# Moved weight steps, gate and fills, and fewer zero matmuls, in the first rounds of an RWKV and Sinkhorn-MoE kernel

## The chip, the cores and the metric

The kernel runs on one core of a Trainium2 chip. The metric is device time in microseconds (us) of one execution of the whole program. Besides the plain runs there is one profiled execution, from which every row below comes. Its engines are TensorE (PE, its weight loads PEld), VectorE (DVE), ScalarE (ACT), GpSimd (POOL) and SyncE (SP), whose queue issues most of the DMA transfers.

## What is computed

Attention in the RWKV manner over `r`, `k`, `v` of shape (4, 8, 768, 48), and on its output `x` of shape (3072, 384) a mixture of 8 experts whose gate is normalised by 8 Sinkhorn steps:

```python
for t in range(S):
    cur = einsum('bhd,bhe->bhde', u * k[t], v[t])
    y[t] = einsum('bhd,bhde->bhe', r[t], state + cur)
    state = w * state + einsum('bhd,bhe->bhde', k[t], v[t])
x = y as (3072, 384)
logits = x @ w_gate
P = exp(logits - logits.max())
for _ in range(8):
    P /= P.sum(1, keepdims=True) + 1e-9
    P /= P.sum(0, keepdims=True) + 1e-9
    P *= N / E
out = sum over e of P[:, e] * (relu(x @ w1[e]) @ w2[e])
```

## The kernel before, in words

The program has an attention part of 27 rounds (the loop at L720, `i` from 0), in which the 24 tiles of 128 tokens pass a software pipeline, and then 14 stages for experts 1 to 7. From the sixth round on (`i` = 5) TensorE also works on expert 0: `units` is a list of groups of matmuls that `work` (L693) takes one by one. In rounds 1 to 5 there are no units yet, and `work` issues three zero matmuls instead (`spin`, L286: 128x512, f16, into a PSUM tile that nobody reads, `pz`). Everything is issued in program order: `InOrder` (L21) keeps each engine's instructions in the order in which the Python code calls them, so the order of the calls is the order on every engine's queue.

What a round `i` does, by function:

- `load_chunk(i + 4)` puts three loads on SP's queue (`rn`, `kn`, `vn`, 192 KB each). `prep(i + 2)` (L477) scales r on POOL (`rp`) and k on VectorE (`kp`). `bonus_dot(i + 1)` (L483) is two products on POOL, r times k and that times u (`rk`).
- `stage_b(i + 1)` (L500) transposes `rp` and `kp` on TensorE (`prT`, `pkT`); ScalarE copies them out (`rT`, `kT`).
- `scale_x(i - 2)` scales an output tile on ScalarE (`xsc`). `bonus(i)` (L490) is a reduction on VectorE (`dg`) and two products on POOL, the second of which reads `hbx`.
- `stage_c(i)` (L511) makes the scores on TensorE (`pA`), which VectorE copies through a mask into `at`, and the state's update (`pu`, then `S`).
- `stage_e(i - 2, bank_)` (L576) transposes a scaled tile (`px`); ScalarE writes its high half into `hbx` (a CAST) and VectorE the low half. `stage_d(i - 1)` (L547) makes the output (`py`); VectorE adds the bonus (`x`) and takes the scale of each row from its maximum (`xm`, `inv_s`, `xs`). `stage_f(i - 3, bank_)` (L584) multiplies by the gate's weights (`px<-wgp,hbx`); VectorE writes `lparts`.

The tiles `prT`, `pkT`, `pA`, `pu` and `py` share four PSUM banks in turn (pool `ps3`), so a round's second `pA` tile takes the bank of an earlier `py` and must wait until VectorE has read that for `x`.

Between these the round places the preparation of expert 0's weights: `split_weights` (L151) gives a list of steps, and `STEPS` (L708) says how many of them `prepare` (L689) takes after `stage_c` and at the round's end. For w1, and again for w2, they are: three maxima (`amax`, VectorE, `wm`), `reduce_max` (`wma`), an empty step, `across` (a transpose, then a reduction and a small matmul that spreads the maximum over the partitions), an empty step, `scale` (`isw`, `sw`), and for each of three pieces a high half on ScalarE (`high`: `ws<-ws,sw`, 128x1024) and a low half on VectorE (`low`: `ws<-ws,sw,ws`). The gate's weights `wg` pass the same steps once: `gate_max` (`wgm`), `gate_across`, `gate_split` (`iswg`, `swg`, then `wgp` on ScalarE and VectorE).

Before the loop, the two `at` tiles are cleared on POOL (L355), part of `hbx` is zeroed on ScalarE (L334), and a branch (L409) on a flag sends rare decay values down a slow path, which is not taken here. SP issues no load past that branch until the first loads of w1 have landed.

Of the kernel before, what the change touches and what calls it, by code (L numbers as in the profile page):

```python
# [8 lines left out]
F32 = mybir.dt.float32  # L9
# [3 lines left out]
ALU = mybir.AluOpType  # L13
# [19 lines left out]
def rwkv_sinkhorn_moe(  # L33
# [17 lines left out]
    B, H, S, D = r.shape  # L51
# [99 lines left out]
    def split_weights(e, r1, r2, home):  # L151
        w1h = part(home, F16, 0, (KC, F))
        w1l = part(home, F16, KC * F, (KC, F))
        w2h = part(home, F16, 2 * KC * F, (FC, DM))
        w2l = part(home, F16, 2 * KC * F + FC * DM, (FC, DM))
        isw = const.tile([P, 2], F32, name=f"isw_{e}")
        sw = sm.tile([P, 2], F32, tag="sw", name=f"sw_{e}")
        m = sm.tile([P, 2 * KC], F32, tag="wm", name=f"wm_{e}")
        ma_ = [sm.tile([P, 1], F32, tag=f"wma{j}", name=f"wma_{e}_{j}") for j in range(2)]
        res = {}  # L160
        pieces = []

        def rest_():
            pass

        for raw, wh, wl, j in ((r1, w1h, w1l, 0), (r2, w2h, w2l, 1)):
            fl = [x.rearrange("p c f -> p (c f)") for x in (raw, wh, wl)]
            n = fl[0].shape[1] // KC

            def amax(i, fl=fl, j=j, n=n):  # L170
                V.tensor_reduce(
                    m[:, j * KC + i : j * KC + i + 1], fl[0][:, i * n : (i + 1) * n],
                    axis=AX.X, op=ALU.max, apply_absolute_value=True,
                )

            def reduce_max(j=j):
                V.tensor_reduce(ma_[j], m[:, j * KC : (j + 1) * KC], axis=AX.X, op=ALU.max)

            def across(j=j):
                res[j] = over_partitions(ma_[j], 1, ps1, "ph", f"w{e}_{j}")  # L180
                next(res[j])

            def scale(j=j):
                pow2_scale(next(res[j]), isw[:, j : j + 1], sw[:, j : j + 1], 0.25)

            def high(i, fl=fl, j=j, n=n):
                sl = slice(i * n, (i + 1) * n)
                S_.activation(fl[1][:, sl], fl[0][:, sl], AF.Copy, scale=sw[:, j : j + 1])

            def low(i, fl=fl, j=j, n=n):  # L190
                sl = slice(i * n, (i + 1) * n)
                V.scalar_tensor_tensor(
                    fl[2][:, sl], fl[0][:, sl], sw[:, j : j + 1], fl[1][:, sl],
                    op0=ALU.mult, op1=ALU.subtract,
                )

            steps = [lambda i=i, f=amax: f(i) for i in range(KC)] + [reduce_max, rest_, across, rest_, scale]
            for i in range(KC + 1):
                fs = [lambda i=i, f=high: f(i)] if i < KC else []
                fs += [lambda i=i, f=low: f(i - 1)] if i else []  # L200
                if i >= KC - 1:
                    fs.append(lambda i=i, j=j: split_done.add((("w1", "w2")[j], i - KC + 1)))
                steps.append(lambda fs=fs: [f() for f in fs])
            pieces += steps
        return (w1h, w1l, w2h, w2l, isw), pieces
# [113 lines left out]
    for c in range(KC):  # L319
# [11 lines left out]
    V.memset(unit[:, :, 0:1], 1.0)  # L331
    V.memset(step[:, :, 0:1], 0.0)
    V.memset(hbx[:, HB : 2 * HB], 0.0)
    S_.mul(  # L334
        hbx[:, 2 * HB :].rearrange("p (a q) -> p a q", q=HP),
        unit[:, :1, 1:].broadcast_to([P, HB // HP, HP]), 0.0,
    )
    spin(19)
    wbd = ac.tile([P, NPAIR, 2, D], F32, name="wbd")
    G.memset(wbd, 0.0)  # L340
# [11 lines left out]
    at_ = [ac.tile([P, H, C], F32, name=f"at{i}") for i in range(2)]  # L352
    for t_ in rp_ + kp_:
        G.memset(t_[:, :, D:], 0.0)
    for t_ in at_:  # L355
        G.memset(t_, 0.0)

    wlim = part(hb3, F32, 2496, (H, D))[:1]
    flag = ac.tile([1, 1], F32, name="flag")
# [51 lines left out]
            scan_channels(scratch)  # L411

    load_part(1, "v", v)
    load_part(3, "r", r)
    load_part(3, "k", k)
    Q.dma_start(wg, w_gate.rearrange("(c p) e -> p c e", p=P))
    load_part(2, "v", v)
    load_part(3, "v", v)

# [14 lines left out]
    V.tensor_tensor(tab[:, :, HP:], pw[:, :, :HP], gb, op=ALU.mult)  # L434
    V.tensor_tensor(tab[:, :, :HP], iv[:, :, HP:0:-1], gb, op=ALU.mult)
    S_.copy(tabr[:, :, :HP], pw[:, :, HP - 1 :: -1])
    S_.copy(tabr[:, :, HP:], iv[:, :, 1:])
    rtab = ac.tile([P, NPAIR, 2, HP], F32, name="rtab")
    ktab = ac.tile([P, NPAIR, 2, HP], F32, name="ktab")
# [42 lines left out]

    def bonus_dot(tt):  # L483
        ld_ = loads[tt]
        rk = at2.tile([P, H, D], F32, tag="rk", name=f"rk_{tt}", bufs=3)
        G.tensor_tensor(rk, ld_["r"], ld_["k"], op=ALU.mult)
        G.tensor_tensor(rk, rk, ub, op=ALU.mult)
        st[tt]["rk"] = rk

# [203 lines left out]
    def work(n, ready=True):  # L693
        if not ready:
            spin(3)
            return
        for _ in range(n):
            if units:
                whole(units.pop(0))
# [3 lines left out]
    for sg in range(3):  # L703
# [2 lines left out]
        side += steps  # L706

    STEPS = {  # L708
        0: (2, 1), 1: (1, 2), 2: (2, 1), 3: (1, 1), 4: (1, 0),
        5: (1, 1), 6: (2, 2), 7: (3, 1), 8: (1, 1),  # L710
    }

    def n_steps(i):
# [4 lines left out]
    stage_b(0)  # L718
    bonus_dot(0)
    for i in range(NTT + 3):  # L720
        if i == 2:
            gate_max()
        if i + 2 < NTT:
            if i + 4 < NTT:
                load_chunk(i + 4)
            if i == 0:
                Q.dma_start(raws[1], w2[0].rearrange("(c p) d -> p c d", p=P))
            prep(i + 2)
        if i + 1 < NTT:
            bonus_dot(i + 1)  # L730
            stage_b(i + 1)
        if 2 <= i <= NTT + 1:
            scale_x(i - 2)
        work(1, i > 4)
        if i < NTT:
            bonus(i)
            if ("S", i) in st:
                st[i]["S"] = st.pop(("S", i))
            stage_c(i)
        for _ in range(n_steps(i)[0]):  # L740
            prepare()
        if i <= NTT:
            work(2 if i > 8 else 1, i > 4)
        if i == 2:
            gate_res = gate_across()
        if i >= 2:
            bank_ = ps2.tile([P, TB], F32, tag="po", name=f"px_{i}")
        if 2 <= i <= NTT + 1:
            stage_e(i - 2, bank_)
            emitted[0] = i - 1  # L750
        if i > NTT:
            work(2)
        if 1 <= i <= NTT:
            stage_d(i - 1)
        if i == 2:
            gate_split(gate_res)
        for _ in range(n_steps(i)[1]):
            prepare()
        if 3 <= i:
            stage_f(i - 3, bank_)  # L760
        done = i - 2
        if 0 <= done < NTT and done % TH == TH - 1:
            po_ = done // TH
            if po_ == 0:
                units += [g1_unit(0, fc, W) for fc in range(FC)]
                units += [g2_half(0, t, 0, W) for t in range(TH)]
                pend = [(0, t, 1) for t in range(TH)]
            for j in range(2 if po_ else 0):
                g1 = [g1_unit(po_, fc, W) for fc in range(j * FHC, (j + 1) * FHC)]
                g2 = [g2_half(*a, W) for a in pend]  # L770
                units += merged(g1, g2)
                pend = [(po_, t, j) for t in range(TH)]
# [447 lines left out]
```

## Time and profile before

| | |
|---|---|
| runs | 1563.62, 1563.85, 1565.07 us; median 1563.85 us |
| the profiled execution | 1563.49 us, of which the span from first to last instruction is 1561.8 us |
| PE | 1549.8 us busy (99%), 9297 matmuls |
| DVE | 1020.8 us (65%) |
| ACT | 671.9 us (43%) |
| POOL | 589.0 us (38%) |
| chain of waits that ended last | PE 95%, DVE 2%, POOL 1% |
| granted TensorE clock | 1.0 in all 40 slices |

The table is read as one long stretch in which TensorE is never free, with a short beginning in which other engines hold it up. Shares over the whole span hide that beginning: the rows further down look at it by itself.

### The profile page before, as it was taken

What the parts mean: (1) busy time and instruction counts of PE and PEld (TensorE: products, weight loads), DVE (VectorE), ACT (ScalarE), POOL (GpSimd) and SP (SyncE); (2) the same over time, 40 slices, a digit from 0 to 9 for tenths busy, and PEclk for the clock granted to TensorE, in tenths of its full rate; (3) what the DMA queues carried; (4) which work ended last, traced back from release to release, by engine and by line L of the source; (5) the groups of instructions that cost most, each with busy time, mean ns of one, the idle gap of its engine ahead of it and who ended that gap; (6) DMA issues with size and microseconds to landing.
All of it is one profiled execution on the core that took longest, in us unless ns stands there. A gap on an engine that the chain in (4) does not pass through costs nothing.

```text
span 1561.8 us, 24068 instructions
## 1 busy us (share of the span) xinstructions
PE 1549.8 (99%) x9297; PEld 899.0 (58%) x9297; DVE 1020.8 (65%) x1694; ACT 671.9 (43%) x1190; POOL 589.0 (38%) x688
## 2 busy tenths in 40 slices
PE   8999999999999999999999999999999999999999
PEld 5877786655555555555555555555555555555555
DVE  7876674957666676666666666666666656656554
ACT  3433332534444354544444453544444444535320
POOL 8777764620012424243342424242423324242200
PEclk9999999999999999999999999999999999999999
DMA  9333311221215556576766666565545555556434
GB/s 197 68 88 79 84 49 36 98 82 45 92 64 103 79 87 111 85 127 90 128 83 122 86 127 90 93 95 70 86 57 99 57 95 61 96 59 97 56 91 132
DMA packets 167638, 138.26 MB, mean 89 GB/s; under 512 B 90337, under 2 KB 161762, under 8 KB 167522
## 3 DMA queue, kind: packets, MB, share of 16 engines
q0 software_dynamic: 44928, 61.36, 32.6%
q1 hardware_dynamic: 122384, 75.35, 17.4%
q8 instruction: 73, 1.20, 0.3%
q14 instruction: 43, 0.35, 0.1%
q10 hardware_dynamic: 210, 0.00, 0.0%
HBM read 55.39 MB, written 80.23 MB: 87 GB/s over the span
## 4 chain that ended last, share of the span: by engine, by line
PE 95%; DVE 2%; POOL 1%; ACT 0%; issue 0%; DMA 0%; SPq 0%; POOLq 0%; DVEq 0%; ACTq 0%
PE po L29 47%; PE bZ L29 11%; PE bY L29 11%; PE ph L29 5%; PE bA L29 5%; PE bB L29 5%; PE py L29 3%; PE bC L29 2%; PE pA L29 1%; PE pu L29 1%; PE px L29 1%; PE prT L29 1%; POOL rk L29 1%; PE pkT L29 1%; DVE tb L29 0%
## 5 line engine op out<-in xcount | busy, mean ns | idle before, releaser
L29 PE MATMUL po<-ws,hbx 128*128 128x384 f16 x3360 | 736.8, 326 | 0.0
L29 POOL DMA_DIRECT2D accd<-stg x288 | 249.7, 867 | 695.4 <-ACT stg L29 681.1
L29 PEld LDWEIGHTS <-hbx 128*128 128x128 f16 x3504 | 336.3, 98 | 292.7 <-issue 1.3
L29 PEld LDWEIGHTS <-ws 128*128 128x128 f16 x3096 | 302.4, 98 | 243.8 <-issue 1.4
L29 ACT ACTIVATE hbx<-tb 128x512 f16<-128x512 f32 x224 | 141.0, 630 | 450.0 <-DVE tb L29 450.0
L29 PE MATMUL po<-ws,hb 128*128 128x384 f16 x1248 | 322.8, 326 | 0.0
L29 DVE TENSOR_TENSOR tb<-bY,tb 128x512 f32<-128x512 f32 x168 | 116.1, 691 | 195.6 <-PE bY L29 195.4
L29 ACT ACTIVATE stg<-po,pe 128x384 f32<-128x384 f32 x312 | 179.1, 574 | 121.8 <-PE po L29 94.9
L29 PE MATMUL bZ<-xv,ws 128*128 128x512 f16 x840 | 227.0, 379 | 0.4 <-DVE tb L29 0.4
L29 PE MATMUL bY<-xv,ws 128*128 128x512 f16 x840 | 227.0, 379 | 0.0
L29 DVE TENSOR_TENSOR tb<-bZ,tb 128x512 f32<-128x512 f32 x168 | 115.5, 688 | 136.0 <-PE bZ L29 136.0
L29 PEld LDWEIGHTS <-hb 128*128 128x128 f16 x1248 | 121.9, 98 | 93.0
L29 POOL TENSOR_TENSOR ucb<-rawb 128x256 f32<-128x256 f32 x84 | 75.8, 953 | 118.0 <-DMA rawb<-in_moe_w_dram 118.0
L29 DVE TENSOR_TENSOR tb<-bB,tb 128x512 f32<-128x512 f32 x112 | 77.4, 691 | 49.2 <-PE bB L29 47.3
L29 PE MATMUL ph<-hbx,ws 128*128 128x384 f16 x576 | 104.3, 326 | 0.5 <-DVE hb L29 0.5
L29 DVE SCALAR_TENSOR_TENSOR hb<-tb,hbx 128x512 f16<-128x512 f32 x112 | 77.2, 689 | 24.6 <-ACT hbx L29 19.5
L29 PE MATMUL bA<-xv,ws 128*128 128x512 f16 x336 | 90.8, 379 | 0.0
L29 PE MATMUL bB<-xv,ws 128*128 128x512 f16 x336 | 90.8, 379 | 0.0
L29 DVE SCALAR_TENSOR_TENSOR hbx<-tb,hbx 128x512 f16<-128x512 f32 x112 | 77.9, 695 | 14.7 <-ACT hbx L29 10.4
L29 DVE SCALAR_TENSOR_TENSOR hb<-ph,hb 128x384 f16<-128x384 f32 x64 | 35.3, 553 | 40.7 <-ACT hb L29 40.5
L29 ACT COPY tb<-bZ 128x512 f32<-128x512 f32 x56 | 32.7, 585 | 65.6 <-PE bZ L29 65.6
L29 ACT ACTIVATE hb<-ph 128x384 f16<-128x384 f32 x64 | 31.2, 489 | 59.7 <-PE ph L29 58.7
(165 smaller groups left out, 1613.7 us busy)
## 6 DMA issues: line engine op xcount, KB each, us to landing
accd<-stg POOLq DMA_DIRECT2D x288, 192.0 KB, 3.7
rawb<-in_moe_w_dram SPq DMA_DIRECT2D x28, 768.0 KB, 7.1
e0d<-stg SPq DMA_DIRECT2D x48, 192.0 KB, 1.9
hb<-e0d SPq DMA_DIRECT2D x48, 192.0 KB, 3.7
rn<-in_r_dram SPq DMA_DIRECT2D x24, 192.0 KB, 3.2
kn<-in_k_dram SPq DMA_DIRECT2D x24, 192.0 KB, 3.6
vn<-in_v_dram SPq DMA_DIRECT2D x24, 192.0 KB, 2.8
accd<-stg SPq DMA_DIRECT2D x24, 192.0 KB, 1.8
```

What stands on the lines that cost most here:

```text
L29: return lambda *a, **k: self.tc.keep_in_program_order(f(*a, **k))
```

## The change

It has these parts.

- **Fills.** The two `at` tiles are zeroed by ScalarE (a new helper `fill`, the same instruction as that for `hbx`, 128x1024 each) and no longer by POOL. The first product r times k of tile 0 is issued on POOL before the branch, and `bonus_dot(0)` only multiplies it by u.
- **Gate.** The load of `wg` goes ahead of the loads of r and k of tile 3. `gate_max` and `gate_across` run in round 2 (`i` = 1), and `gate_split` in round 3 ahead of the weight steps and of `stage_e`.
- **Weight steps.** The high halves of a weight's first two pieces are steps of their own and come before any low half. There are six such steps for each weight where there were four; `STEPS` gives other counts.
- **Order and zero matmuls.** In round 1 `stage_b(1)` comes after `stage_c(0)`. In rounds 2 to 5 the three zero matmuls between `stage_b` and `stage_c` are gone (12 in all); those between `stage_c` and `stage_e` stay.

```diff
             steps = [lambda i=i, f=amax: f(i) for i in range(KC)] + [reduce_max, rest_, across, rest_, scale]
-            for i in range(KC + 1):
-                fs = [lambda i=i, f=high: f(i)] if i < KC else []
-                fs += [lambda i=i, f=low: f(i - 1)] if i else []
...
+            steps += [lambda i=i, f=high: f(i) for i in range(2)]
+            for i in range(KC):
+                fs = [lambda i=i, f=high: f(i + 2)] if i + 2 < KC else []
+                if fs:
+                    steps.append(lambda fs=fs: fs[0]())
+                fs = [lambda i=i, f=low: f(i)]
...
+    def fill(x_):
+        n = x_.shape[1]
+        S_.mul(
+            x_.rearrange("p (a q) -> p a q", q=HP),
+            unit[:, :1, 1:].broadcast_to([P, n // HP, HP]), 0.0,
+        )
...
-    for t_ in at_:
-        G.memset(t_, 0.0)
+    fill(at_[0].rearrange("p h c -> p (h c)"))
+
+    rk0 = at2.tile([P, H, D], F32, tag="rk", name="rk_0", bufs=3)
+    G.tensor_tensor(rk0, loads[0]["r"], loads[0]["k"], op=ALU.mult)
...
     load_part(1, "v", v)
+    Q.dma_start(wg, w_gate.rearrange("(c p) e -> p c e", p=P))
     load_part(3, "r", r)
     load_part(3, "k", k)
-    Q.dma_start(wg, w_gate.rearrange("(c p) e -> p c e", p=P))
...
     S_.copy(tabr[:, :, :HP], pw[:, :, HP - 1 :: -1])
+    fill(at_[1].rearrange("p h c -> p (h c)"))
     S_.copy(tabr[:, :, HP:], iv[:, :, 1:])
...
     STEPS = {
-        0: (2, 1), 1: (1, 2), 2: (2, 1), 3: (1, 1), 4: (1, 0),
-        5: (1, 1), 6: (2, 2), 7: (3, 1), 8: (1, 1),
+        0: (2, 1), 1: (1, 2), 2: (4, 2), 3: (1, 1), 4: (0, 1),
+        5: (1, 1), 6: (1, 2), 7: (4, 2), 8: (1, 1),
     }
...
-        if i == 2:
+        if i == 1:
             gate_max()
...
+        if i + 1 < NTT and i:
             stage_b(i + 1)
         if 2 <= i <= NTT + 1:
             scale_x(i - 2)
-        work(1, i > 4)
+        if i > 4 or i == 0:
+            work(1, i > 4)
...
             stage_c(i)
+        if i == 2:
+            gate_split(gate_res)
+        if i == 0:
+            stage_b(1)
         for _ in range(n_steps(i)[0]):
             prepare()
         if i <= NTT:
             work(2 if i > 8 else 1, i > 4)
-        if i == 2:
+        if i == 1:
             gate_res = gate_across()
...
-        if i == 2:
-            gate_split(gate_res)
         for _ in range(n_steps(i)[1]):
             prepare()
```

How this moves instructions is shown at three places. In the names, the number after the tile is the round's tile, and the last number only tells buffers apart.

ScalarE in round 3 (`i` = 2) before, from the scaling of tile 0 (`xsc_0`) on; `hbx<-px_2` is the high half of tile 0, `ws1<-ws0` a high half of a piece of w1:

```order
L29 ACTIVATE xsc_0_501<-x_0_461,xs_0_465 128x384
L29 CAST hbx_72<-px_2_545 128x3x128
L29 ACTIVATE wgp_307<-wg_119,swg_305 128x3x8
L29 ACTIVATE ws1_75<-ws0_74,sw_0_309 128x1024
L29 COPY rT_4_595<-prT_4_590 128x512
L29 COPY kT_4_602<-pkT_4_597 128x512
```

And the same place now:

```order
L29 ACTIVATE xsc_0_503<-x_0_464,xs_0_468 128x384
L29 ACTIVATE wgp_309<-wg_119,swg_307 128x3x8
L29 ACTIVATE ws1_75<-ws0_74,sw_0_311 128x1024 x2
L29 CAST hbx_72<-px_2_545 128x3x128
L29 ACTIVATE ws1_75<-ws0_74,sw_0_311 128x1024
L29 COPY rT_4_590<-prT_4_585 128x512
L29 COPY kT_4_597<-pkT_4_592 128x512
```

The write of tile 0's high half has moved from ahead of the gate and the weights to behind the gate's half and two high halves of w1.

ScalarE in round 8 (`i` = 7) before, with `hb3<-ph_0_4` and `hb3<-ph_0_5` the outputs of two of expert 0's groups, and here a high half of w2 between them:

```order
L29 ACTIVATE xsc_5_1014<-x_5_968,xs_5_972 128x384
L29 ACTIVATE hb3_73<-ph_0_4_1016 128x384
L29 ACTIVATE ws1_75<-ws0_74,sw_0_309 128x1024
L29 ACTIVATE hb3_73<-ph_0_5_1057 128x384
L29 CAST hbx_72<-px_7_1069 128x3x128
```

And now:

```order
L29 ACTIVATE xsc_5_998<-x_5_952,xs_5_956 128x384
L29 ACTIVATE hb3_73<-ph_0_4_1000 128x384
L29 ACTIVATE ws1_75<-ws0_74,sw_0_311 128x1024 x2
L29 ACTIVATE hb3_73<-ph_0_5_1042 128x384
L29 CAST hbx_72<-px_7_1054 128x3x128
```

Two high halves stand between the two outputs where one stood.

SP's queue right behind the branch, before:

```order
L29 DMA vn_1_253<-in_v_dram 128x8x48
L29 DMA rn_3_255<-in_r_dram 128x8x48
L29 DMA kn_3_257<-in_k_dram 128x8x48
L29 DMA wg_119<-in_moe_w_gate_dram 128x3x8
L29 DMA vn_2_260<-in_v_dram 128x8x48
```

And now:

```order
L29 DMA vn_1_254<-in_v_dram 128x8x48
L29 DMA wg_119<-in_moe_w_gate_dram 128x3x8
L29 DMA rn_3_257<-in_r_dram 128x8x48
L29 DMA kn_3_259<-in_k_dram 128x8x48
L29 DMA vn_2_261<-in_v_dram 128x8x48
```

The gate's small load has passed the loads of r and k of tile 3.

## Rows read from the trace of the kernel before

**Rows 1.** Busy time by stretch: start:end, us, then busy us (count) for each engine

```profile
16.00:52.00 36.00, 33.20 (x300) 27.79 (x299) 30.41 (x64) 11.53 (x20) 32.49 (x31) 1.00 0.75 150
52.00:1558.00 1506.00, 1504.35 (x8952) 865.37 (x8948) 977.55 (x1609) 653.09 (x1162) 546.25 (x638) 1.00 0.49 86
```

**Rows 2.** Timeline of TensorE: start us, us, instructions, [idle before <-what ended it]

```profile
11.39 1.06 PE L29 MATMUL pt_tab<-ident,hb 128*128 128x128 f32 x8 [2.07 <-DVE wc L29]
...
35.33 0.81 PE L29 MATMUL pz<-zeros 128*128 128x512 f16 x3
...
38.82 1.13 PE L29 MATMUL pu<-vn,kp 128*128 128x96 f32 x8 [1.59 <-ACT rT L29]
...
43.38 0.29 PE L29 MATMUL px<-wgp,hbx 128*128 128x16 f16 x6
...
49.08 1.91 PE L29 MATMUL py<-vn,at 128*128 128x48 f32 x16
51.80 0.29 PE L29 MATMUL px<-wgp,hbx 128*128 128x16 f16 x6 [0.81 <-DVE hbx L29]
...
78.19 0.29 PE L29 MATMUL px<-wgp,hbx 128*128 128x16 f16 x6 [0.31 <-DVE hbx L29]
```

**Rows 3.** Timeline of POOL in the first rounds

```profile
12.72 2.28 POOL L29 TENSOR_TENSOR rp<-rn,rtab 128x384 f32<-128x384 f32 x2 [4.98 <-DMA ws<-in_moe_w_dram]
14.97 1.31 POOL L29 TENSOR_TENSOR rk<-rn,kn 128x384 f32<-128x384 f32 x1
...
22.38 1.01 POOL L29 TENSOR_TENSOR rp<-rn,rtab 128x384 f32<-128x384 f32 x1
```

**Rows 4.** Timeline of ScalarE before the rounds

```profile
3.10 2.81 ACT L29 ACTIVATE hbx<-hb 128x3072 f32<-128x3072 f32 x1
8.86 0.41 ACT L29 COPY hb<-hb 128x256 f32<-128x256 f32 x1 [2.95 <-DVE hb L29]
10.67 0.40 ACT L29 COPY hb<-hb 128x256 f32<-128x256 f32 x1 [1.41 <-DVE hb L29]
```

**Rows 5.** Loads of r (16 to 18 us) and wg (18 to 20 us): issue ns, start

```profile
L29 SPq DMA_DIRECT2D rn<-in_r_dram x1: 505/505/505, 17.0 to 17.0; - x1
DMA to landing us min/median/max: 4.9/4.9/4.9
...
L29 SPq DMA_DIRECT2D wg<-in_moe_w_gate_dram x1: 697/697/697, 18.4 to 18.4; - x1
```

**Rows 6.** Timeline of VectorE in rounds 1 to 5

```profile
17.58 0.55 DVE L29 TENSOR_REDUCE dg<-rk 128x8 f32<-128x384 f32 x1 [0.90 <-POOL rk L29]
...
23.13 0.68 DVE L29 TENSOR_TENSOR kp<-kn,ktab 128x384 f32<-128x384 f32 x1
...
31.44 0.16 DVE L29 RECIPROCAL sw<-isw 128x1 f32<-128x1 f32 x1
...
34.28 0.56 DVE L29 TENSOR_TENSOR hbx<-px,hbx 128x384 f16<-128x384 f32 x1 [2.26 <-ACT hbx L29]
...
37.29 0.43 DVE L29 SCALAR_TENSOR_TENSOR wgp<-wg,swg,wgp 128x24 f16<-128x24 f32 x1 [0.38 <-ACT wgp L29]
...
41.73 0.55 DVE L29 TENSOR_TENSOR hbx<-px,hbx 128x384 f16<-128x384 f32 x1
...
49.84 1.45 DVE L29 SCALAR_TENSOR_TENSOR ws<-ws,sw,ws 128x1024 f16<-128x1024 f32 x1
```

**Rows 7.** Timeline of ScalarE in rounds 3 and 8

```profile
33.77 0.48 ACT L29 CAST hbx<-px 128x384 f16<-128x384 f32 x1 [5.33 <-POOL rk L29]
...
75.56 1.15 ACT L29 ACTIVATE ws<-ws,sw 128x1024 f16<-128x1024 f32 x1 [3.22 <-DVE sw L29]
76.61 0.47 ACT L29 ACTIVATE hb<-ph 128x384 f16<-128x384 f32 x1
```

**Rows 8.** Zero matmuls alone in two stretches: start:end, us, busy (count), granted clock

```profile
1.30:6.40 5.10, 5.09 (x12) 1.00 0.88 150
6.80:9.00 2.20, 2.20 (x12) 1.00 1.14 183
```

More of the change, by code (lines that the diff above doesn't have):

```diff
@@ L197, in split_weights @@
             steps = [lambda i=i, f=amax: f(i) for i in range(KC)] + [reduce_max, rest_, across, rest_, scale]
-            for i in range(KC + 1):
-                fs = [lambda i=i, f=high: f(i)] if i < KC else []
-                fs += [lambda i=i, f=low: f(i - 1)] if i else []
-                if i >= KC - 1:
-                    fs.append(lambda i=i, j=j: split_done.add((("w1", "w2")[j], i - KC + 1)))
+            steps += [lambda i=i, f=high: f(i) for i in range(2)]
[4 more added lines that the diff above has]
+                fs = [lambda i=i, f=low: f(i)]
+                if i:
+                    fs.append(lambda i=i, j=j: split_done.add((("w1", "w2")[j], i - 1)))
                 steps.append(lambda fs=fs: [f() for f in fs])
@@ L333, in rwkv_sinkhorn_moe @@
     V.memset(hbx[:, HB : 2 * HB], 0.0)
[L334 to L337, printed above, removed]
+    def fill(x_):
[4 more added lines that the diff above has]
+        )
+    fill(hbx[:, 2 * HB :])
     spin(19)
@@ L484, in bonus_dot @@
         ld_ = loads[tt]
-        rk = at2.tile([P, H, D], F32, tag="rk", name=f"rk_{tt}", bufs=3)
-        G.tensor_tensor(rk, ld_["r"], ld_["k"], op=ALU.mult)
+        rk = rk0
+        if tt:
+            rk = at2.tile([P, H, D], F32, tag="rk", name=f"rk_{tt}", bufs=3)
+            G.tensor_tensor(rk, ld_["r"], ld_["k"], op=ALU.mult)
         G.tensor_tensor(rk, rk, ub, op=ALU.mult)
```

## The prediction

> **What bounds the kernel now.** I read busy time by stretch first [rows 1]. From 52 us on TensorE works 1504 of 1506 us, and the change takes no TensorE work out of that stretch; so nothing that only speeds up VectorE, ScalarE or POOL there can matter. Before it, from 16 to 52 us, TensorE is busy for 33.2 of 36 us, POOL for 32.5 and VectorE for 30.4: three engines are nearly full, and each holds up the others. What the change can alter is when TensorE leaves this beginning, and how long it stands idle in the few places after it. TensorE's timeline shows both [rows 2]. It waits 1.59 us at 38.82 for ScalarE and 0.81 us at 51.80 for VectorE's last write of `hbx`; from 51.80 on it runs full, but for 0.31 us at 78.19. So the two numbers to forecast are the time at which the `px<-wgp,hbx` of 51.80 starts, and the idle time at 78.19. The clock reads full speed throughout.
>
> **The change part by part.**
>
> Fills. Before the rounds POOL waits 4.98 us for `rtab` [rows 3], so its two clears cost nothing where they were. On ScalarE a fill of 1024 columns is a third of the one of 3072 that took 2.81 us, some 1.0 us each [rows 4]; one goes into an idle stretch of 2.95 us, the other into one of 1.41 us. Cost nothing; without these gaps it would be 2 us. The first r times k, 1.31 us on POOL [rows 3], moves into the same 4.98 us of waiting: POOL reaches its `rp` of tile 3 at 22.38 - 1.31 = 21.1.
>
> Loads. That `rp` needs r of tile 3. The load was issued at 17.0 and landed 4.9 us later, at 21.9 [rows 5]; now the load of `wg` is issued ahead of it, which took SP 0.70 us where it stood. So it lands between 21.9 and 22.6, and `rp` starts there: POOL's 1.3 us are given back on the spot. Of k of tile 3 the trace has no landing; it was issued behind r, so not before 21.9, and VectorE's `kp` at 23.13 did not wait for it [rows 6]. VectorE loses its wait of 0.90 us at 17.58 and would come to this `kp` at about 22.2, `wgm` included. I put it at 22.9, nearer to 23.13 because `wg` is ahead of both loads; between 22.2 and 23.8.
>
> Gate and scale. Before, 8.5 us lay between the start of that `kp` and the end of `sw` (31.60) [rows 6]. The gate's steps now come in between: five small ones of about 0.16 us by the row of `sw`, and `wgp` with its wait, 0.38 + 0.43; together 1.6. So `sw` is ready at 22.9 + 8.5 + 1.6 = 33.0.
>
> ScalarE in round 3. Before, the CAST to `hbx` started at 33.77, when POOL had finished reading that place [rows 7]. Now two high halves stand ahead of it and cannot start before `sw`. One takes 1.15 us, the next instruction starting 1.05 after it [rows 7]: the CAST goes at 33.0 + 2.1 = 35.1, its partner on VectorE at 35.6 and not 34.28 [rows 6], 1.3 us later. Behind it on VectorE stands `x`, and behind that, for its PSUM bank, TensorE's second score tile of round 4; TensorE idles there for some 2.5 us, where before it had three zero matmuls [rows 2] and little idle time.
>
> To the next write of `hbx`. From 34.28 to 41.73 are 7.45 us [rows 6]. The gate's 1.3 (three small steps, the wait, `wgp`) have left this piece, and one more low half (1.45 us by its row, 1.4 start to start) has come in: 7.5, so 43.1, and done at 43.7. TensorE's `px<-wgp,hbx` of 43.38 [rows 2] waits for that: 0.3 us later than before. ScalarE's `rT`, which it waited for at 38.82, is no longer late by itself, since the score tile ahead is.
>
> Round 5. Behind that `px` TensorE has one set of zero matmuls less, 0.81 us with a last drain that overlaps [rows 2], 0.7 net; and VectorE has one low half less ahead of the write that ended the wait of 0.81 us, so this wait goes too. TensorE comes to the place of 51.80 at 51.80 + 0.3 - 0.7 - 0.8 = 50.6. VectorE has written `hbx` at 51.75 + 0.3 - 1.4 = 50.65: about even. A gain of 1.2 us.
>
> The other zero matmuls. The sets of rounds 2 to 4 go at points where TensorE then waits for VectorE; they are worth nothing, as long as VectorE is late. If it is not, they are worth 0.7 each, at most 2.1 more.
>
> Maxima of w2 one round earlier: VectorE gets one 128x1024 reduction more around 51 us and one less a round later. Over the long stretch it is busy for 978 of 1506 us [rows 1], so I take 0; upper bound one such instruction waiting in full, 1.2 (an estimate between 1.0, a ScalarE fill of this size, and 1.45, a low half).
>
> Round 8. The high half at 75.56 takes 1.15 us, ScalarE's output of the second group stands behind it until 76.61 [rows 7], then VectorE, then TensorE, which idles 0.31 us at 78.19 [rows 2]. Now there are two high halves: 1.05 us more of idle time. TensorE is full before and after, so nothing hides it, except that a part may go if `sw` comes earlier: 0.7 to 1.1, and I take 1.0. The third high half and the low halves come later in gaps as before.
>
> Sum: -1.2 + 1.0 = -0.2 us. The profiled execution took 1563.49 us (span 1561.8 and 1.7 around it), which makes 1563.3; the median of the runs shown lies 0.36 above it, so the forecast is **1563.6 us**: no change that can be told. Throughout, 0.2% (3.1 us) is what a measurement of this kernel can tell from none.
>
> **A rule against it.** Zero matmuls do no work; their use can only be the clock. In the first stretch twelve of them take 5.09 us, 0.42 each, and later twelve take 2.20 [rows 8]: the array started at 1.2 GHz and went to 2.4 only after 5 us of unbroken work, although the granted clock reads 1.00 in both. On the other side, after 2.07 us of idling at 11.39 eight transposes took 1.06 us, no sign of the lower level [rows 2]. The idle stretch that I expect in round 4 is 2.5 us long, just outside what the trace shows to be harmless. The Trainium skill (TensorE: Matmul & The Clock Gate, "Why this matters for your kernels") warns of idle gaps between bursts of matmuls, after which the clock returns to its lower level; by that rule the removed sets would be paid for there. No row of this trace shows such a fall.
>
> **The rivals.**
>
> The clock falls in round 4 (slower). Place: the wait for `x` of tile 1. It decides if the fall happens at all: then at least 5.1 us run at half speed as at the start, which loses 2.5 us; at most all of TensorE's work until the f16 products of round 6 is doubled, some 13 us. Time 1566 to 1577, nearest 1568, as the dense work of round 6 ends it early. For it: the start; against it: 11.39. Chance 0.12.
>
> The loads behind `wg` come late. If k of tile 3 lands at 23.8, everything up to 51 us moves by 0.9 and the gain shrinks to 0.3: 1564.5. For it: SP is the gate here, and three loads wait behind `wg`; against it: `wg` is 12 KB beside 192 KB each. Chance 0.14.
>
> VectorE is not late. If k lands at 22.2 and the scale is ready early, the gain in the beginning is 2 us, and if the two high halves of round 8 cost little, the time is 1561.6. With all 2.1 us of the other zero matmuls as well it is near 1560. For it: TensorE has 2.4 us of waits to lose in rows 2; against it: two high halves stand ahead of the CAST by construction. Chance 0.14.
>
> The forecast itself: 0.60, with 1562.5 to 1564.7 from the bounds above.
>
> **How the numbers follow.** The range has to hold eight in ten. 1560.9 to 1566.8 takes in the forecast, the late loads, nearly all of the third rival and the cheapest end of the clock; it leaves out most of the clock's 0.12 and some 0.03 below. Faster by over 0.2% (under 1560.7) needs all of the third rival: 0.05. Slower (over 1567.0) is the clock with more than its least price: 0.10. The rest, 0.85, is within.
>
> **What would show it.** Right: POOL's `rp` of tile 3 starts within 0.5 us of 22.4 in spite of the earlier r times k; the CAST to `hbx` in round 3 stands behind two high halves and starts near 35; the `px<-wgp,hbx` of 51.80 starts near 50.6; the idle time at the place of 78.19 is about 1.3 us. Wrong: eight transposes that take 2 us instead of 1.1, or zero matmuls of 0.4 us, anywhere after 16 us (the clock); a start of round 6 before 49.5 or after 52; or idle time of TensorE after 80 us that was not there before.

## The result, and the profile after

The changed kernel takes **1567.37 us** (median of 20 runs, 1565.99 to 1569.82). The kernel before, run beside it on the same chip, takes 1564.05 (20 runs, 1563.47 to 1567.68). The ratio of the two is 1.0021, 95% interval 1.0015 to 1.0027: slower by 3.3 us, just over the 0.2% that can be told from no change, and outside the range of the prediction. The profiled execution of the changed kernel took 1567.40 us, its span 1565.7, which is 3.9 more than before. All 20 runs show a mean granted clock below full, 0.993 to 0.998.

The stretches first, as in [rows 1]: start:end, us, then busy us (count) of TensorE, its weight loads, VectorE, ScalarE and POOL, the granted clock, DMA share and GB/s. The two lines of [rows 1] come first, then pieces of the beginning.

```profile
16.00:52.00 36.00, 31.55 (x248) 27.30 (x245) 28.95 (x61) 11.52 (x19) 28.81 (x27) 0.86 0.71 151
52.00:1558.00 1506.00, 1503.34 (x8957) 866.03 (x8956) 977.08 (x1610) 653.70 (x1163) 548.75 (x640) 1.00 0.49 86
...
24.00:26.00 2.00, 0.41 (x4) 0.28 (x3) 2.00 (x4) 0.00 (x0) 1.92 (x3) 0.99 1.04 207
26.00:28.00 2.00, 1.27 (x7) 1.27 (x8) 1.93 (x7) 0.01 (x1) 1.92 (x3) 0.50 1.23 196
...
30.00:32.00 2.00, 2.00 (x14) 1.78 (x13) 1.24 (x3) 0.00 (x0) 1.92 (x3) 0.50 1.05 392
...
34.00:46.00 12.00, 10.14 (x90) 9.24 (x89) 8.91 (x18) 5.89 (x9) 8.53 (x8) 1.00 0.56 108
46.00:48.00 2.00, 1.73 (x13) 1.65 (x13) 1.86 (x7) 0.36 (x1) 2.00 (x3) 0.61 0.34 70
48.00:50.00 2.00, 2.00 (x19) 1.67 (x17) 2.00 (x3) 1.32 (x3) 1.92 (x2) 0.54 0.15 24
50.00:80.00 30.00, 30.00 (x275) 25.12 (x271) 24.18 (x54) 10.33 (x19) 19.33 (x21) 1.00 0.37 72
```

The granted clock, 1.00 throughout before, is 0.50 from 26 to 32 us and about half again from 46 to 50: TensorE works at 1.2 GHz there. Forty slices of a page are too coarse for it; the page prints 90% or more in every slice, and only a table of short stretches shows the falls. Both come when TensorE was idle for long (0.41 us busy of 2 just ahead of the first).

TensorE's timeline, start us, busy us, instructions, [idle before <-what ended it], at the places of [rows 2] and at the falls:

```profile
10.78 1.06 PE L29 MATMUL pt_tab<-ident,hb 128*128 128x128 f32 x8 [2.07 <-DVE wc L29]
...
26.73 0.37 PE L29 MATMUL pmax_w<-ident,wma 128*1 128x128 f32 x1 [2.32 <-DVE wma L29]
26.90 1.06 PE L29 MATMUL prT<-ident,rp 128*128 128x128 f32 x4
...
30.75 2.02 PE L29 MATMUL pu<-vn,kp 128*128 128x96 f32 x8
...
38.66 1.16 PE L29 MATMUL pA<-rT,kT 64*128 64x128 f32 x14 [0.33 <-DVE x L29]
...
46.27 0.37 PE L29 MATMUL px<-wgp,hbx 128*128 128x16 f16 x6 [1.81 <-DVE hbx L29]
46.51 1.09 PE L29 MATMUL prT<-ident,rp 128*128 128x128 f32 x4
...
54.72 0.29 PE L29 MATMUL px<-wgp,hbx 128*128 128x16 f16 x6
...
82.14 0.29 PE L29 MATMUL px<-wgp,hbx 128*128 128x16 f16 x6 [1.34 <-DVE hbx L29]
```

Three waits stand out. At 26.73 TensorE waits 2.32 us for `wma`, the maximum of w1; behind it four transposes take 1.06 us and the eight `pu` 2.02, where eight took 1.13 before [rows 2]. At 46.27 it waits 1.81 us for `hbx`, and four transposes take 1.09 again. The `px<-wgp,hbx` of 51.80 [rows 2] now starts at 54.72, **2.92 us later**. At the place of 78.19 it idles 1.34 us and not 0.31, **1.03 more**. 2.92 and 1.03 are 3.95, the whole difference of the two spans.

What lies behind the first wait and between the two falls is on VectorE's timeline:

```profile
23.89 0.56 DVE L29 TENSOR_TENSOR kp<-kn,ktab 128x384 f32<-128x384 f32 x1 [1.53 <-DMA kn<-in_k_dram]
...
30.85 1.36 DVE L29 COPY_PREDICATED at<-mask,pA 128x512 f32<-128x512 int32 x2 [0.76 <-PE pA L29]
32.87 0.56 DVE L29 TENSOR_TENSOR S<-pu,S 128x384 f32<-128x384 f32 x1 [0.67 <-PE pu L29]
...
34.80 0.17 DVE L29 RECIPROCAL sw<-isw 128x1 f32<-128x1 f32 x1
37.58 0.56 DVE L29 TENSOR_TENSOR hbx<-px,hbx 128x384 f16<-128x384 f32 x1 [2.62 <-ACT hbx L29]
```

VectorE waits 1.53 us for k of tile 3, and `wma` stands behind that: this makes TensorE's first long wait. With the clock at half, VectorE waits for TensorE in its turn (0.76 and 0.67), so `sw` is ready at 34.97, and ScalarE's two high halves and its CAST come after that, as its timeline shows here and in round 8 (places of [rows 7]):

```profile
35.00 2.19 ACT L29 ACTIVATE ws<-ws,sw 128x1024 f16<-128x1024 f32 x2 [0.77 <-DVE sw L29]
37.09 0.46 ACT L29 CAST hbx<-px 128x384 f16<-128x384 f32 x1
...
78.47 2.19 ACT L29 ACTIVATE ws<-ws,sw 128x1024 f16<-128x1024 f32 x2 [3.22 <-DVE sw L29]
80.57 0.47 ACT L29 ACTIVATE hb<-ph 128x384 f16<-128x384 f32 x1
```

### The profile page after: what moved, and what is told of

Read it like the earlier page. It is cut to its first block, busy times and chain, and to the rows that moved or that the text cites. A ratio compares the mean times of both kernels' runs of the same rounds, so it can differ in the third digit from the quotient of the medians.

```text
span 1565.7 us, 24042 instructions
## 1 busy us (share of the span) xinstructions
PE 1551.1 (99%) x9285; PEld 901.7 (58%) x9285; DVE 1020.1 (65%) x1694; ACT 674.2 (43%) x1192; POOL 587.7 (38%) x686
## 4 chain that ended last, share of the span: by engine, by line
PE 95%; DVE 3%; ACT 0%; issue 0%; DMA 0%; DVEq 0%; ACTq 0%
PE po L29 47%; PE bZ L29 11%; PE bY L29 11%; PE ph L29 5%; PE bA L29 5%; PE bB L29 5%; PE py L29 3%; PE bC L29 2%; PE pA L29 1%; PE pu L29 1%; PE prT L29 1%; PE px L29 1%; PE pkT L29 1%; DVE at L29 0%; DMA kn<-in_k_dram 0%
```

## The experiments

The theory: the moved steps make TensorE wait longer, the clock falls in those waits, and round 8 adds its 1.03 us. Its rivals: the missing zero matmuls alone make the falls; the waits cost by themselves and the clock falls in time that was lost anyway; the load of `wg` makes it all late. Medians of the experiments (9 to 11 runs each), each with its ratio to the kernel before on the same chip:

| run | from | edit | median us | ratio, 95% interval |
|---|---|---|---|---|
| e1_zeros_back | after | the 12 zero matmuls back | 1567.82 | 1.0022 [1.0011, 1.0032] |
| e2_zeros_out | before | the 12 zero matmuls out | 1567.09 | 1.0018 [1.0008, 1.0027] |
| e3_one_high | after | one high half less ahead, round 8 | 1565.08 | 1.0009 [1.0000, 1.0019] |
| e15_one_high_3 | after | the same, round 3 | 1565.51 | 1.0008 [0.9999, 1.0017] |
| e9_one_high2 | after | the same, both rounds | 1564.20 | 1.0001 [0.9992, 1.0010] |
| e7_zeros_one_high | after | both rounds, zero matmuls back | 1564.36 | 1.0004 [0.9995, 1.0013] |
| e5_cover | after | other zero matmuls, in the waits | 1567.54 | 1.0018 [1.0009, 1.0027] |
| e8_cover_one_high | after | e5 and e9 together | 1563.37 | 0.9995 [0.9986, 1.0004] |
| e14_two_high_8 | after | e8, round 8 as in the change | 1564.35 | 1.0004 [0.9995, 1.0013] |
| e13_cover_8 | after | e14, zero matmuls in round 8's wait | 1564.16 | 0.9996 [0.9987, 1.0005] |
| e10_wg_late | after | load of `wg` back in its place | 1567.82 | 1.0023 [1.0014, 1.0032] |
| e12_cover_wg_late | after | e8 and e10 together | 1564.33 | 1.0003 [0.9994, 1.0012] |
| e4_fills | before | the fills of the change alone | 1564.56 | 0.9998 [0.9989, 1.0008] |
| e6_fills_start | before | e4, zero matmuls at the start | 1564.76 | 1.0001 [0.9992, 1.0010] |
| e11_fills_cover | before | e6, zero matmuls in two more waits | 1563.14 | 0.9996 [0.9987, 1.0005] |

### The zero matmuls, put back and taken out (e1, e2)

```diff
# e1, from the changed kernel; e2 is the reverse, from the kernel before
-        if i > 4 or i == 0:
-            work(1, i > 4)
+        work(1, i > 4)
```

> The changed kernel with the 12 zero matmuls of rounds 2 to 5 put back, all else as changed. Theory of the clock (TensorE's clock falls because these matmuls are gone, and the halved clock makes the time): the granted clock stays at 1.00 from 16 us on, the px<-wgp,hbx that starts at 54.72 us in the changed kernel starts near 51.5, and the time is 1564.4 us (1563.7 to 1565.2), 3 us less than changed; the wait of 1.3 us in round 8 stays. Rival (the new waits make the time: late loads, and two high halves ahead of the CAST; the clock only follows them): the waits are still there with or without zero matmuls, the start stays after 53.5 and the time is 1566 to 1567.5 us.

> The kernel before without the 12 zero matmuls, nothing else changed. Theory of the clock: it falls here too, at least once between 20 and 52 us, and the time is 1565.5 to 1568 us. Rival (the new waits): without the moved steps there is nothing to wait for, the clock stays, and one set of zero matmuls less on the path makes 1563 to 1563.9 us.

With the zero matmuls back the changed kernel gains nothing (1567.82). TensorE's timeline and the stretches of e1 say why: they stand behind the waits, not in them, and the three at 28.26 take 1.43 us where three took 0.81 [rows 2].

```profile
26.38 0.37 PE L29 MATMUL pmax_w<-ident,wma 128*1 128x128 f32 x1 [1.45 <-DVE wma L29]
...
28.26 1.43 PE L29 MATMUL pz<-zeros 128*128 128x512 f16 x3
```

```profile
26.00:28.00 2.00, 1.62 (x8) 1.62 (x9) 1.89 (x7) 0.35 (x1) 1.92 (x4) 0.52 1.21 221
...
46.00:48.00 2.00, 2.00 (x16) 1.60 (x16) 1.86 (x6) 0.93 (x2) 2.00 (x3) 0.64 0.04 7
```

The clock falls at the same two places. In the order of the kernel before it is otherwise: there the removal alone costs 3.1 us. Its waits of 1.59 and 0.81 [rows 2] grow to 1.84 and 1.45, as TensorE comes to them earlier, and the clock falls at the first: the eight `pu` behind it take 1.88 us and not 1.13. An earlier fall follows the wait at 11.39, now 2.97 us (2.07 before): eight transposes take 1.63 us where they took 1.06. The profiled execution, 1565.69 us, is one of the three fastest of the 11. TensorE's timeline and a stretch of e2:

```profile
11.39 1.63 PE L29 MATMUL pt_tab<-ident,hb 128*128 128x128 f32 x8 [2.97 <-DVE wc L29]
...
38.84 1.88 PE L29 MATMUL pu<-vn,kp 128*128 128x96 f32 x8 [1.84 <-ACT rT L29]
...
53.48 0.29 PE L29 MATMUL px<-wgp,hbx 128*128 128x16 f16 x6 [1.45 <-DVE hbx L29]
```

```profile
40.00:42.00 2.00, 2.00 (x8) 1.24 (x8) 1.17 (x2) 0.83 (x1) 1.19 (x2) 0.50 0.02 3
```

So work taken off TensorE ahead of a wait is not worth nothing: it lengthens the wait, and the clock can make it dear. But for this change as it stands, the missing zero matmuls are not the cause.

### One high half less ahead of ScalarE's outputs (e3, e15, e9, e7)

```diff
# e9; e3 has the second line alone, e15 the first; e7 is e9 with the edit of e1
-        0: (2, 1), 1: (1, 2), 2: (4, 2), 3: (1, 1), 4: (0, 1),
-        5: (1, 1), 6: (1, 2), 7: (4, 2), 8: (1, 1),
+        0: (2, 1), 1: (1, 2), 2: (3, 3), 3: (1, 1), 4: (0, 1),
+        5: (1, 1), 6: (1, 2), 7: (3, 3), 8: (1, 1),
```

> The changed kernel, but in round 8 only one high half of w2 ahead of the second group's output (counts of that round 3 and 3 where they were 4 and 2). Both theories: TensorE's idle time in round 8 goes from 1.34 back to 0.3 us and the time falls by 1.0 us against the changed kernel, to 1566.4 us. Rival: the time is made up for elsewhere and stays at 1567.4 us.

> The changed kernel with steps 3 and 3 in the round at 35 us alone; round 8 as in the change, no zero matmuls added. Theory (both places cost, and the costs add up: the round at 35 us 0.9, by e3_one_high at 1565.1 against e9_one_high2 at 1564.2; round 8 2.3): 1567.37 - 0.9 = 1566.5. Rival (the round at 35 us costs nothing once round 8 is as in the change, since falls of the clock come at most one for some stretch): 1567.4.

> The changed kernel with steps 3 and 3 in place of 4 and 2 in both rounds (at 35 us and at 78 us), the zero matmuls left out as in the change, and no others added. Theory (ScalarE's order and the missing zero matmuls each make the clock fall, in different waits): the wait for wma at 26.73 stays above 1.5 us and the clock falls there in part of the runs; the wait for hbx in round 4 is shorter than 1.81; time between that of e7_zeros_one_high and that of e3_one_high, 1564.4 to 1565.1. Rival (ScalarE's order alone makes the loss): 1563.4, as with the waits covered.

> The changed kernel with the removed zero matmuls back and one high half less ahead of ScalarE's CAST in the rounds at 35 us and at 78 us (steps 3 and 3 in place of 4 and 2). Theory of the prediction (the order on ScalarE makes the wait for hbx in round 4): the CAST of 37.09 comes 1.1 us earlier, the wait of 1.82 us at 45.84 goes to under 1, the clock doesn't fall there, and the time is near 1564. Rival (the wait comes from VectorE's order of work, gate and low halves ahead of hbx): the wait stays above 1.4 us, the clock falls, and only the 1.03 us of round 8 come back: 1566.8.

This is the edit that brings the time back: four numbers in a table, and of the 3.3 us lost none is left that can be told (1564.20). The clock alone does not make the loss: all 11 runs of e9 have a mean clock below full too (0.993 to 0.999), and ten of them lie at 1564.62 or below. The idle time in round 8 is 0.31 us again in e3 (at 81.38), as it is in the line of e8 further down (at 77.93).

By their medians against the change's 1567.37, round 8 alone gives back 2.3 us (1.0 was expected), round 3 alone 1.9 (0.9 was expected), both 3.2; that the two add up to more than the pair is within the intervals, some 1.5 us to either side. Each gives back more than the length of its wait (1.03 us in round 8), and e13 and e14 below show for round 8 what the rest is. In e9 the first wait stays (1.93 us for `wma`) and that for `hbx` shrinks to 1.41 (from 1.81); the clock is down at the table's transposes already, behind a longer wait than the change's 2.07. TensorE's timeline of e9:

```profile
10.78 1.41 PE L29 MATMUL pt_tab<-ident,hb 128*128 128x128 f32 x8 [2.55 <-DVE wc L29]
```

The zero matmuls change nothing here either: e7 with them and e9 without are 0.2 us apart. For e7 a wait under 1 us had been expected; it was 1.40, so the order on ScalarE is one part of that wait and VectorE's work the rest. e7's profile also shows this order with the clock up to the end (1563.22 us): through both waits it holds 1.00, and the place of 51.80 comes at 51.36. A stretch and TensorE's timeline of e7:

```profile
16.00:52.00 36.00, 32.72 (x295) 27.76 (x292) 31.31 (x64) 11.92 (x20) 31.18 (x30) 1.00 0.70 150
```

```profile
26.49 0.27 PE L29 MATMUL pmax_w<-ident,wma 128*1 128x128 f32 x1 [1.53 <-DVE wma L29]
...
43.83 0.37 PE L29 MATMUL px<-wgp,hbx 128*128 128x16 f16 x6 [1.40 <-DVE hbx L29]
...
51.36 0.29 PE L29 MATMUL px<-wgp,hbx 128*128 128x16 f16 x6
```

### Zero matmuls in the waits themselves (e5, e8)

```diff
# e5, from the changed kernel; e8 is this and the edit of e9
# spin is also given, where it is called with them, the pool and the tag of its tile
...
-    spin(5)
+    spin(12)
...
+            if i == 1:
+                spin(5)
+            if i == 3:
+                spin(5, ps1, "ph")
         if 3 <= i:
             stage_f(i - 3, bank_)
```

> The changed kernel with other zero matmuls put into TensorE's waits: twelve in place of five ahead of the table's transposes, five in front of pmax_w (where the changed kernel waits 2.32 us at 26.73) and five in front of the px of round 4 (1.81 us at 46.27); the twelve that the change removed stay out. Theory (the clock's two falls make the difference, and the waits only bring them on): the granted clock stays at 1.00 from 12 us on, and the time is near 1564.5 (1563.8 to 1565.2), what is left over the kernel before being the 1.03 us of round 8. Rival (VectorE and ScalarE come late by themselves, and the clock falls in time that TensorE had to wait anyway): the clock stays up and the px at 54.72 still starts after 54, time 1566 or more.

> The changed kernel with zero matmuls in the waits as in e5_cover and steps 3 and 3 in both rounds as in e7_zeros_one_high. Theory (clock plus round 8 is all that the change costs): 1563.4, equal to the kernel before or up to 0.7 us faster by the fills. Rival (waits themselves cost): 1565 or more.

e5 missed, and is the most telling run. Its clock did stay up past 26 us, so what I had predicted for rounds 3 and 4 could happen undisturbed. ScalarE's timeline:

```profile
35.88 0.46 ACT L29 CAST hbx<-px 128x384 f16<-128x384 f32 x1
```

and then on TensorE:

```profile
37.44 1.72 PE L29 MATMUL pA<-rT,kT 64*128 64x128 f32 x14 [1.94 <-DVE x L29]
...
81.65 0.29 PE L29 MATMUL px<-wgp,hbx 128*128 128x16 f16 x6 [1.34 <-DVE hbx L29]
...
83.14 2.86 PE L29 MATMUL ph<-hbx,ws 128*128 128x384 f16 x9
```

with this stretch:

```profile
38.00:45.00 7.00, 7.00 (x37) 6.02 (x35) 6.92 (x11) 1.44 (x3) 5.89 (x5) 0.52 0.34 65
```

Covering two waits moved the fall to the next two that were not covered: the wait for `x` of tile 1 and that of round 8, behind which nine f16 products took 2.86 us (1.63 at full clock, in the kernel before). Neither theory nor rival of e5 had said so; the rival's time (1567.54) and place (the `px` of 54.72 at 54.22) came out, but not with the clock up, as it had it. In e8, where one high half less also shortens these two (0.90 and 0.31 us), all 11 runs lie between 1562.54 and 1563.88, and the profiled one holds 1.00 to the end. TensorE's timeline of e8:

```profile
26.59 0.27 PE L29 MATMUL pmax_w<-ident,wma 128*1 128x128 f32 x1 [1.21 <-DVE wma L29]
...
36.34 1.16 PE L29 MATMUL pA<-rT,kT 64*128 64x128 f32 x14 [0.90 <-DVE x L29]
...
51.24 0.29 PE L29 MATMUL px<-wgp,hbx 128*128 128x16 f16 x6 [0.24 <-DVE hbx L29]
...
77.93 0.29 PE L29 MATMUL px<-wgp,hbx 128*128 128x16 f16 x6 [0.31 <-DVE hbx L29]
```

### Round 8: the wait, and the clock behind it (e13, e14)

```diff
# e13, from e8; e14 has the first edit alone
-        5: (1, 1), 6: (1, 2), 7: (3, 3), 8: (1, 1),
+        5: (1, 1), 6: (1, 2), 7: (4, 2), 8: (1, 1),
...
+            if i == 7:
+                spin(6, ps1, "ph")
```

> e8_cover_one_high with the change's two high halves ahead in round 8 again (steps 4 and 2), and six zero matmuls in front of the px for which TensorE then waits. Theory (the wait in round 8 costs its 1.03 us, and the fall of the clock behind it is a second price that zero matmuls take away): 1563.4 + 1.0 = 1564.4, mean clock 1.000 in nearly all runs. Rival (only the wait costs, the clock has no part in round 8): the same 1564.4 with and without these zero matmuls.

> As e13_cover_8, without the six zero matmuls. Theory: a part of the runs at 1564.4 and a part with a fall of the clock in round 8, 1.7 us more (half of a fall of 3.41 us), so a median between 1564.4 and 1566.1 and runs above 1566. Rival: all at 1564.4.

With zero matmuls in the wait all 11 runs lie between 1563.85 and 1564.65, with a mean clock of 0.999 to 1.000: 0.8 us over e8, which is the wait's own price, near the 1.03 of its length. Without them six runs lie there (1563.78 to 1564.35) and five 1.1 us or more above (1565.45 to 1568.18), at a mean clock of 0.997 to 0.999. The medians hardly differ (1564.16 and 1564.35), the spread does: the second price is paid in a part of the runs. In e14's own profile the clock held, so that the fall of its dear runs lies behind this wait is not seen there: it is read from e5, and from e13, which differs by the six zero matmuls alone and has no dear run. TensorE in e13, where the wait is filled, then in e14:

```profile
78.83 0.29 PE L29 MATMUL px<-wgp,hbx 128*128 128x16 f16 x6
```

```profile
78.73 0.29 PE L29 MATMUL px<-wgp,hbx 128*128 128x16 f16 x6 [1.33 <-DVE hbx L29]
```

### The load of wg behind r and k again (e10, e12)

```diff
     load_part(1, "v", v)
-    Q.dma_start(wg, w_gate.rearrange("(c p) e -> p c e", p=P))
     load_part(3, "r", r)
     load_part(3, "k", k)
+    Q.dma_start(wg, w_gate.rearrange("(c p) e -> p c e", p=P))
```

> The changed kernel with the load of wg back behind the loads of r and k of tile 3, everything else as in the change. Theory (the load's place makes k of tile 3 late, and with it wma and TensorE's wait of 2.32 us at 26.73): k's product on VectorE starts 0.5 us earlier or more, that wait shrinks to 1.9 or less, the time falls by 0.5 to 1 us to about 1566.6. Rival (VectorE's order, with the gate's maximum and the maxima of w1 ahead, sets wma): the wait stays within 0.2 us of 2.32, and the time at 1567.4, because the gate's maximum now waits for wg on VectorE.

> e8_cover_one_high with the load of wg back behind the loads of r and k of tile 3. Theory (with the clock up, an earlier k shortens the waits of the rounds): 1563.0, 0.4 us less. Rival (the next load or the gate takes the place of the wait): 1563.4, no change.

Both theories missed; the rival of e10 had the time right (1567.4, measured 1567.82) and the reason, but not the place of the wait. VectorE's `kp` came no earlier, since its gate maximum now waits ahead of it, as VectorE's timeline of e10 shows:

```profile
23.84 0.18 DVE L29 TENSOR_REDUCE wgm<-wg 128x1 f32<-128x24 f32 x1 [1.95 <-DMA wg<-in_moe_w_gate_dram]
23.93 0.64 DVE L29 TENSOR_TENSOR kp<-kn,ktab 128x384 f32<-128x384 f32 x1
```

And TensorE's wait moved forward, to v of tile 1, which landed late in this run: 1.71 us ahead of `pu` at 22.47, with the clock down behind it. The time stays, or is longer in the covered version (e12, 1564.33 against e8's 1563.37). With the gate one round earlier some load is late for VectorE in either order; the place of `wg` is not the cause.

### The kernel before with parts of the change, and a better version (e4, e6, e11)

```diff
# e4, the fill helper as in the change; e6 adds the second edit, e11 all
...
-    for t_ in at_:
-        G.memset(t_, 0.0)
+    fill(at_[0].rearrange("p h c -> p (h c)"))
...
+    fill(at_[1].rearrange("p h c -> p (h c)"))
...
-    spin(5)
+    spin(12)
...
+            if tt == 3:
+                spin(5, ps1, "ph")
             for p_ in range(NPAIR):
                 T.matmul(
                     pu[:, p_, :], kp[:, p_, :],
...
+        if i == 4:
+            spin(4, ps1, "ph")
         if 3 <= i:
```

> The kernel before with the fills alone moved from POOL to ScalarE. In the changed kernel the transposes of the table started at 10.78 us where before they started at 11.39, and VectorE's wsafe took 0.17 us where it took 0.78. If POOL's clears held VectorE up, the same happens here: 10.8 us and 0.17 us; the total then is 1563.3 us if the 0.6 us last, and 1563.9 us if the loads of tile 3 (landing at 21.9 us) take them back. If the 0.6 us came from elsewhere, the start stays at 11.4 us.

> The kernel before with the two fills on ScalarE and twelve zero matmuls in place of five ahead of the table's transposes, nothing else of the change. Theory (runs of the kernel before that are some 2 us above its fastest had the clock fall after TensorE's idle stretch at 11.39, and the zero matmuls close that stretch): nearly all runs lie at 1562.9 with a mean clock of 1.000. Rival (the falls of those runs come later, in the waits of the rounds): runs at 1562.9 and at 1565 as with the fills alone, median near 1564.5.

> The kernel before with the two fills on ScalarE and zero matmuls in TensorE's three waits: twelve in place of five ahead of the table's transposes, five in front of pu of tile 3 (the wait of 1.59 us at 38.82) and four in front of the px of 51.80; nothing else of the change. Theory (the runs of the kernel before above its fastest are falls of the clock in these waits, and the fills give 0.5 us): all runs at 1562.9 with a mean clock of 1.000. Rival (the zero matmuls there delay the work that ends the waits, or the falls come elsewhere): median 1563.9 or more.

The runs of e4 fall into two groups: five at 1562.87 to 1563.05 with a mean clock of 1.000, six at 1564.56 to 1565.22 with 0.998 or 0.999. The kernel before, run beside it, has three: eight runs at 1563.47 to 1563.69 with 1.000, nine at 1563.84 to 1563.99 and thirteen at 1565.45 to 1565.74, these two with 0.998 or 0.999. So the kernel before loses the clock in part of its runs too, and at the same mean clock this goes with 0.4 us in some and with 2.0 in others. The fills are worth 0.6 us where the clock stays up, hidden in the median by the groups. Covering the idle stretch at the start changed nothing (e6). Its profile has the fall later, where `hbx` is waited for, with four transposes of 1.09 us behind it on TensorE:

```profile
51.20 0.30 PE L29 MATMUL px<-wgp,hbx 128*128 128x16 f16 x6 [0.81 <-DVE hbx L29]
51.36 1.09 PE L29 MATMUL prT<-ident,rp 128*128 128x128 f32 x4
```

Covering the two waits at 38.82 and 51.80 [rows 2] left seven of 11 runs at 1562.89 to 1563.64. e11's median, 1563.14, is the lowest of all; against the kernel before it can't be told from no change, and four of its runs still lie at 1565.06 or more. Where the clock falls in those was not seen.

## Why the prediction was wrong

**Fills: mis-sized.** Forecast at nothing, they gave 0.6 us at the table's transposes (11.39 [rows 2] to 10.78). VectorE's first step on the decay (`wsafe`) had taken 0.78 us with POOL's clears running beside it (5.90 to 7.74); with the clears gone the same step takes 0.17, in the change and in e4. I had asked only whether POOL had time for the clears, not whom they held up. VectorE and POOL before, then VectorE after:

```profile
6.98 0.78 DVE L29 TENSOR_SCALAR wsafe<-wt 128x4 f32<-128x4 f32 x1 [0.75 <-DVE flag L29]
...
5.90 1.84 POOL L29 MEMSET at<- 128x1024 f32 x2
```

```profile
6.98 0.17 DVE L29 TENSOR_SCALAR wsafe<-wt 128x4 f32<-128x4 f32 x1 [0.75 <-DVE flag L29]
```

**r times k, and the loads: right in the mechanism, later than the bounds.** POOL's `rp` of tile 3 starts at 23.05 after 2.21 us of waiting for r, forecast 21.9 to 22.6: the landing decides, as forecast. k's product starts at 23.89, forecast 22.9, bound 23.8. The load of r was issued at 18.81, 1.8 us later than before [rows 5], and `wg` ahead of it explains only some 0.7 of that. The rest is SP's first load behind the branch, at 17.68 and not at 16.49. In the profiles of this case it starts between 16.49 and 17.93, at either place of `wg`, so one profile could not fix it. POOL and SP in the change:

```profile
23.05 0.99 POOL L29 TENSOR_TENSOR rp<-rn,rtab 128x384 f32<-128x384 f32 x1 [2.21 <-DMA rn<-in_r_dram]
...
18.81 0.41 SPq L29 DMA_DIRECT2D rn<-in_r_dram  x1
```

**Gate, scale, ScalarE in round 3: mechanism right.** The CAST stands behind two high halves, 2.09 us after the first. It starts at 37.09 and not 35.1: k is late by 1.0 and VectorE waits 1.4 for a TensorE at half clock, and some 0.4 of this is saved on the way. In e5, where the clock held until then, it is 35.88, and TensorE waits 1.94 us for `x`, forecast 2.5.

**The gain at 51.80: sign wrong.** Forecast 1.2 us earlier, measured 2.92 later. With the clock up and one high half less it comes 0.44 earlier in e7 and, with the zero matmuls out, 0.56 earlier in e8 (51.24), and that is what the fills bring. So the moved gate and steps and the missing zero matmuls are worth next to nothing there even undisturbed: in e8 the wait for `hbx` at 51.80 shrank to 0.24 us, but 1.21 for `wma` and 0.90 for `x` took its place. The change's second high half in round 3 makes it worse: the wait for `x` is 1.04 us longer in e5 than in e8, both with the clock up until then.

**Zero matmuls: "worth nothing" holds for the change, by e1 and by e7 against e9, but not as a rule:** e2 shows 3.1 us lost in the order before.

**Maxima of w2:** no new wait was seen there; it was not tried by itself.

**Round 8: right in the profile** (idle 1.34 us, forecast about 1.3), too cheap in the price: 0.8 to 1.0 us always, and a fall of the clock in some runs.

**The step that failed is the clock, which stood in the sum at nothing and had a chance of 0.12.** The prediction named the fall, its sign (transposes that take twice as long) and its price (1566 to 1577, nearest 1568; measured 1567.37). The nearness is in part luck: the place it named was the wait for `x`, where the clock reads 1.00 in the change (34 to 46 us), and the falls came at the waits for `wma` and `hbx`. Its least price, 2.5 us, is above the 0.4 and 2.0 us that go with a lower mean clock in the kernel before. It argued from the 2.07 us at 11.39 that such an idle stretch is harmless. But a fall is a matter of chance from run to run: the same place, with 2.55 us, has the clock down in the profile of e9, and that of e14 holds it through 1.33 us where e5's falls after 1.34. One execution without a fall could not show that a wait is safe. The runs shown ahead of the prediction held a hint: two at 1563.6 to 1563.9, one at 1565.07. And it saw one place for a fall, where the change makes four longer waits (for `wma`, for `x`, for `hbx`, and in round 8); all 20 of its runs lost the clock somewhere, and e5 shows that closing two waits leaves the others.

How the miss divides is an estimate. e13 has the change's round 8 and the clock nearly full in all runs (1564.16); with the 1.04 us of round 3 the change at full clock would take about 1565.2. That is 1.6 above the forecast, by the gain at 51.80 that did not come and the second high half that costs there, and still inside the range. The other 2.2 us, up to 1567.37, would be the clock's, and they carry the time out of it.

The rule of the Trainium skill that the prediction set against the change (TensorE: Matmul & The Clock Gate, "Why this matters for your kernels": the clock falls back after idle gaps between bursts) speaks for the measured outcome. The trace agrees in kind, with 0.50 after a wait of 2.32 us. But the Trainium skill means longer gaps than any single wait here, so the prediction applied the rule to more than it says, and the measurement decides.

**What stays open:** the change with its own counts in round 3 and the clock up to the end was not seen; where the dear runs of e11 and e14 lose the clock; and why e9 keeps its time although its profile (1564.62 us) shows three falls. Perhaps a fall costs little where TensorE must wait soon after it anyway; that would fit e9, and the middle group of the kernel before, but no run here isolates it.

## What to carry to other kernels

A wait of TensorE has two prices, its length and the chance that the clock falls behind it, and the second can be the larger: count how many waits a change lengthens, not only by how much the path moves. The two come together: shortening two of the waits brought the time back although the clock still fell (e9). Before trusting a profile that reads full speed, look at the spread of the runs: the dearest group, some 2 us up, went with a mean clock below full, and comparing the group at full clock with its like showed a gain of 0.6 us that the medians hid. Work placed in front of an engine's output on the way to TensorE (here one high half too many) is paid even where the long stretch has ample idle time on that engine.

## What was not expected of the hardware

POOL's two clears of 128x1024 made a VectorE instruction on 128x4 elements last 0.78 us instead of 0.17 while they ran. And TensorE's clock fell to half at waits from 0.81 us (e6) to 2.55 us (e9, at the place of 11.39) among small matmuls, while it held through 2.07 us ahead of the table's transposes in the change's own profile and through 1.53 us in e7's; by the mean clocks it falls in part of the executions of one kernel and not in others.
